# A gated mix of an S4 convolution and a squared-ReLU layer, forward and backward: the whole kernel written anew around a list scheduler

## The chip, the core and the metric

The kernel runs on one core of a Trainium2 chip. The metric is the device time of one execution in microseconds (us). The engines are named as the profile names them: PE is the matrix engine (PEld its weight loads), DVE the vector engine, ACT the scalar engine, POOL the engine that also issues software DMAs, and SP the engine that here only issues DMAs. The core's 16 DMA engines are shared by all queues.

## The reference

One sequence of L = 2048 rows with D = 448 channels, N = 256 states per channel and F = 1792 hidden units. The result is the output and the gradients of all 14 parameters and inputs, 15 tensors in all.

```python
x = A_u;  g = sigmoid((x * gate_w).sum(-1))
# S4: a kernel K(d, l) of exponentials, and a long convolution
dt = exp(log_dt);  logdA = dt * (A_re + 1j A_im);  dB = dt * (B_re + 1j B_im)
l  = arange(L).astype(bfloat16)              # positions are rounded
K  = einsum("dn,dnl,dn->dl", C, exp(logdA[:, :, None] * l), dB).real
a  = irfft(rfft(pad(u)) * rfft(pad(K)))[:L] + u * Dskip
# dense
h  = relu(x @ w1 + b1);  b = (h * h) @ w2 + b2
out = g * a + (1 - g) * b
# returned: out and the vector-Jacobian product with grad_out
```

Because positions are rounded to bfloat16, only some positions above 256 are distinct. Both kernels write a position as an offset plus a step, and get exp(logdA l) as the product of two tables: X over the offsets, Y over the steps. K is then a matmul of X and Y over the states, and the gradients of the S4 parameters come from the gradient of K by the same tables.

## The kernel before

**Convolution.** The transform is two matmul stages forward (`fwd1` L233, `fwd2` L254) and two back (`inv1` L285, `inv2` L303), with the spectra passing through DRAM (`gd`, `sp`, `hd`) between them. A product of two spectra is four multiplies and two adds on DVE (L268, L271 and others). At the start the kernel transforms u and the gradient, which gives the gradient of K in the rounded positions.

**S4 loop.** 13 offsets (`AOFF`) by 64 steps; 14 chunks of 32 channels, in the loop `for c in range(NCH + 1)`. For each chunk DVE builds X (`step_x`: two multiplies L707 and L708, an add L711) and Y (`double`: L718, L719, L721). `kgen` (L772) makes K by matmuls of 64 steps by 16 columns, and `k_out` stores it in `k_d`. For the gradient X is turned by PE (`tables_t` L798, copied by ACT at L799) and Y by PE (`turn_yt` L810, L811) or by a DMA transpose of SP (`load_yt` L818). `back_z` multiplies the turned Y with the gradient of K (L840), ACT copies the result to SBUF (L844), and `back_p` (L860) multiplies it with X on DVE, two products of 2048 elements, and adds up over offsets by matmuls with a selection matrix (L869). The loop interleaves chunk c's tables with the gradient of chunk c - 1:

```python
for c in range(NCH + 1):
    ...
        ax = build_x(c)
        XTs[c] = [tables_t(c, 0)]
    if c > 0:
        ap = back_p(c - 1, XTs[c - 1][0], back_z(c - 1, YTs[c - 1], (0, 1)), (0, 1), ax)
    ...
            ay = build_y(c, half, ap or ax)
```

**Dense branch.** `hidden` (L551, L554) and the gradient of the hidden layer (L1004 to L1015) run over blocks of 512 rows, `project` (L931) over rows of 128; the blocks `rT_d` and `dhT_d` go to DRAM. They are PE's filler while DVE builds tables.

**Order.** Up to about L1030 the tile framework orders the instructions by the pools' buffers and by priorities. The last part is written out by hand: the generator `units()` loads rows of r and dh (`rows_in` L1039), turns them on PE (`turn` L1044, evacuated L1048), multiplies them (`mul_rows` L1057) and turns the results back (`turn_back` L1074), and steps of it are put between those of the transform of K. That part also reloads K (L1125, L1143), loads the spectra of the products (`load_hs` L294) and the dense branch's rows (L1298), stores the outputs (L1412, L1420, L1422, L1435), and has the parameters' gradients on 128 channels at a time (L1155 to L1202).

Of the kernel before, what the change touches and what calls it, by code (L numbers as in the profile page):

```python
# [19 lines left out]
P = 128  # L20
# [3 lines left out]
DT = 4  # L24
DSZ = [128, 128, 128, 64]
DP = 512
CW = 8
NG = 4
CC = NG * CW
NCH = D // CC  # L30
GC = 2
W2 = 2 * CC
NLEV = 11
RS = 1920
NA = 16
AOFF = [0, 1, 2, 3, 256, 258, 512, 768, 1024, 1280, 1536, 1792, 2048]
VA = len(AOFF)
VROW = 2052
# [64 lines left out]
def position_row(v):  # L103

    m, l0 = (v >> 6) & 3, v & 63
    if v < 512:
        return ((v & 3) >> 1, 8 * (l0 >> 2) + 2 * m + (v & 1)) if v < 256 else (2, 8 * (l0 >> 2) + 2 * m + ((v & 3) >> 1))
    if v < 1024:
        return 3, 8 * (l0 >> 2) + 2 * m + ((v - 512) >> 8)
    return (4, 16 * (l0 >> 3) + 4 * m + ((v - 1024) >> 8)) if v < L else (5, 0)  # L110


def sum_consts():

    mats = {}
    k1 = np.arange(32)
    for l, v in enumerate(rounded_positions()):
        l0 = l % 64
        C = (2.0 / 4096) * np.exp(2j * np.pi * (k1 + 0.5) * l / 4096)
        e, row = position_row(int(v))  # L120
        M = mats.setdefault((l0 % 8, l0 // 16, e, row // 32), np.zeros((2, 32, 2, 32)))
        M[l0 // 8 % 2, :, 0, row % 32] += C.real
        M[l0 // 8 % 2, :, 1, row % 32] -= C.imag
    keys = sorted(mats)
    return np.concatenate([mats[k].reshape(128, 32) for k in keys], axis=1), keys


def rev_dim(ap, k):
    dims = [list(x) for x in ap.ap]
    step, cnt = dims[k]  # L130
    off = ap.offset + step * (cnt - 1)
    dims[k] = [-step, cnt]
    return bass.AP(tensor=ap.tensor, offset=off, ap=dims)


def bcast_dims(ap, spec):

    dims = [list(x) for x in ap.ap]
    out = [dims[0]]
    for s in spec:  # L140
        if isinstance(s, tuple):
            out.append([0, s[1]])
        else:
            out.append(dims[1 + s])
    return bass.AP(tensor=ap.tensor, offset=ap.offset, ap=out)


def sel_host_consts():

    sel = np.zeros((128, 4, 48), np.float32)  # L150
    for i in range(8):
        for a in range(VA):
            r = NA * i + a
            sel[r, 0, 16 + 2 * i] = 1.0
            sel[r, 0, 16 + 2 * i + 1] = 1.0 * AOFF[a]
            sel[r, 2, 16 + 2 * i + 1] = 1.0
    sel[:, 1] = -sel[:, 0]
    sel[:, 3] = -sel[:, 2]
    return sel.reshape(128, 192)

class Ker:
    def __init__(self, tc, pool, psum):
        self.tc = tc
        self.nc = tc.nc
        self.pool = pool
        self.psum = psum
        self.evac_i = 0  # L170
        self.st_i = 0
        self.st_more = []
        self.q2 = tc.nc.gpsimd
        self.q3 = tc.nc.scalar
        self.pair_i = 0
        self.pairs = 3
        self.act_only = False
        self.stage_i = 0
        self.dma_i = 0
        self.n = 0  # L180

    def t(self, tag, shape, dt=bf16, bufs=None):
        self.n += 1
        kw = {} if bufs is None else {"bufs": bufs}
        return self.pool.tile(shape, dt, tag=tag, name=f"{tag}_{self.n}", **kw)

    def ps(self, tag, shape, dt=fp32, bufs=1):
        self.n += 1
        return self.psum.tile(shape, dt, tag=tag, name=f"ps{tag}_{self.n}", bufs=bufs)
# [1277 lines left out]
```

## Time and profile before

| what | value |
| --- | --- |
| runs | 960.9, 983.67, 950.6 us; median 960.9 |
| profiled execution, span | 982.7 us |
| PE / DVE / ACT / POOL busy | 717.6 / 689.9 / 563.8 / 222.4 us |
| mean DMA traffic | 185.60 MB, 189 GB/s |
| last store of K (`k_d`) issued by SP | 698.07 us |

The profile is of one execution. Its span is what the instructions and DMAs of the program cover; the time of that same execution is not listed apart, and among the three runs the one of 983.67 us lies nearest to it. In a row of groups the name left of the arrow is what the instruction writes, the shape follows, then the count, the busy time in us, the mean duration in ns, and the idle time of the engine before these instructions with what ended it.

### The profile page before, as it was taken

To read this page: it belongs to the slowest core of one execution; us is meant where nothing else is said; L and a number is where in the kernel's file an instruction comes from. 1 tells how busy PE (TensorE), PEld (TensorE's weight loads), DVE (VectorE), ACT (ScalarE), POOL (GpSimd) and SP (SyncE) were. 2 spreads that over 40 slices of the span, in tenths; PEclk is the share of its full clock that TensorE was granted. 3 is DMA by queue.
4 is the path that set the end of the run, shared out by engine and by line. 5 is a ranking of instruction groups with operands and counts; after the bars stand their busy time and mean duration, and the time that the engine had idled before them with its cause. 6 is when DMAs were issued, how large, how long until landed. Compare 5 with 4: busy or idle time off the path is not lost. (4 is left out here: it accounts for less than half of the span.)

```text
span 982.7 us, 18887 instructions
## 1 busy us (share of the span) xinstructions
PE 717.6 (73%) x7593; PEld 348.2 (35%) x7593; DVE 689.9 (70%) x1184; ACT 563.8 (57%) x873; POOL 222.4 (23%) x364
## 2 busy tenths in 40 slices
PE   3866456786887587887858688399629688787785
PEld 1322111253433244444333344144415344344242
DVE  4797888648889367978958779489319695675362
ACT  0997467548677467766736456255525487344452
POOL 1340001310121012133132433123324221122112
PEclk9967555797988787896979989788958799899798
DMA  9899746961765866767394955954498999898851
GB/s 189 239 280 346 268 184 245 282 194 55 150 146 138 143 126 120 152 171 166 89 147 120 210 128 150 117 121 118 99 292 239 355 293 302 256 281 256 201 151 33
DMA packets 154354, 185.60 MB, mean 189 GB/s; under 512 B 90900, under 2 KB 127050, under 8 KB 153610
## 3 DMA queue, kind: packets, MB, share of 16 engines
q1 hardware_dynamic: 121158, 85.38, 38.5%
q0 software_dynamic: 24880, 76.81, 27.5%
q10 hardware_dynamic: 8228, 22.20, 6.6%
q8 instruction: 59, 0.97, 0.4%
q14 instruction: 29, 0.24, 0.1%
HBM read 95.13 MB, written 68.97 MB: 167 GB/s over the span
## 5 line engine op out<-in xcount | busy, mean ns | idle before, releaser
L931 PE MATMUL psN<-D,S 128*128 128x448 bf16 x448 | 107.7, 384 | 7.3 <-ACT S L1009 4.5
L844 ACT CAST R<-psF 128x1024 bf16<-128x1024 f32 x56 | 57.0, 1018 | 30.6 <-PE psF L840 30.1
L718 DVE TENSOR_TENSOR Y<-Y,F 128x256 bf16<-128x256 bf16 (+2 forms) x84 | 72.7, 866 | 2.3
L721 DVE TENSOR_TENSOR Y<-Y,F 128x256 bf16<-128x256 bf16 (+2 forms) x84 | 72.6, 865 | 2.1
L860 DVE TENSOR_TENSOR P<-R 128x2048 bf16<-128x2048 bf16 x42 | 50.0, 1219 | 34.1 <-ACT R L844 34.1
L719 DVE TENSOR_TENSOR F<-Y,F 128x256 bf16<-128x256 bf16 (+2 forms) x84 | 71.9, 856 | 0.3
L931 PEld LDWEIGHTS <-S 128*128 128x128 bf16 x448 | 42.3, 103 | 56.3 <-issue 24.1
L1057 PEld LDWEIGHTS <-S 128*128 128x128 bf16 x448 | 43.6, 102 | 51.7 <-issue 23.3
L840 PE MATMUL psF<-R,K 64*32 64x256 bf16 (+1 forms) x672 | 27.6, 345 | 43.6 <-DMA R<-Y 23.9
L1057 PE MATMUL psX<-U,S 128*128 128x448 bf16 x224 | 52.5, 382 | 7.4 <-DVE U L1147 6.1
L1004 PE MATMUL psN<-S,U 128*128 128x512 bf16 x168 | 49.0, 414 | 5.4 <-ACT S L1009 5.4
L1057 PE MATMUL psX<-D,S 128*128 128x449 bf16 x224 | 50.2, 370 | 1.6 <-ACT S L1063 1.3
L707 DVE TENSOR_TENSOR X<-X,F 128x512 bf16<-128x512 bf16 (+1 forms) x70 | 37.5, 536 | 18.0 <-ACT F L741 15.8
L799 ACT COPY R<-psX 128x1024 bf16<-128x1024 bf16 x28 | 28.4, 1015 | 35.5 <-PE psX L798 34.0
L1048 ACT ACTIVATE S<-psN 128x1024 bf16<-128x1024 bf16 x28 | 28.8, 1028 | 31.8 <-PE psN L1044 31.8
L811 ACT COPY M<-psX 128x1024 bf16<-128x1024 bf16 x26 | 26.4, 1015 | 33.5 <-PE psX L810 33.5
L933 POOL DMA_DIRECT2D br_d<-D x32 | 17.7, 554 | 117.7 <-ACT D L932 115.9
L772 PE MATMUL psX<-X,Y 128*64 128x16 bf16 x1792 | 38.8, 181 | 7.1 <-issue 6.4
L551 PE MATMUL psN<-S,U 128*128 128x512 bf16 x120 | 37.0, 423 | 7.6 <-ACT S L557 4.6
L772 PEld LDWEIGHTS <-Y 128*64 128x64 bf16 x1792 | 36.3, 119 | 17.6 <-issue 12.5
L840 PE MATMUL psF<-R,S 64*32 64x256 bf16 (+1 forms) x672 | 32.7, 333 | 11.7 <-issue 9.7
L964 ACT ACTIVATE S<-S 128x1024 bf16<-128x1024 bf16 (+1 forms) x24 | 28.2, 1198 | 21.3 <-DMA S<-rT_d 21.3
(336 smaller groups left out, 1795.5 us busy)
## 6 DMA issues: line engine op xcount, KB each, us to landing
sp<-K ACTq DMA_DIRECT2D x8, 896.0 KB, 4.4
S<-rT_d POOLq DMA_DIRECT2D x8, 896.0 KB, 6.8
dhT_d<-S POOLq DMA_DIRECT2D x28, 256.0 KB, 5.3
S<-rT_d POOLq DMA_DIRECT2D x14, 512.0 KB, 6.7
R<-sp SPq DMA_DIRECT2D x8, 896.0 KB, 10.6
S<-dhT_d POOLq DMA_DIRECT2D x14, 512.0 KB, 4.9
R<-hd SPq DMA_DIRECT2D x16, 448.0 KB, 6.5
rec<-rec_d SPq DMA_DIRECT2D x14, 480.0 KB, 4.3
```

The lines of the kernel that those rows point to most:

```text
L551: T_.matmul(ps[:], lhsT=w1w[:, dt, j * P:j * P + P], rhs=UT[:, dt, 512 * lc:512 * lc + 512], start=(dt == 0), stop=False, skip_group_check ...
L707: V.tensor_tensor(out=hi4, in0=lo, in1=bcast_dims(pr, [0, (None, n), 1]), op=ALU.mult)
L718: V.tensor_tensor(out=hi, in0=lo, in1=bcast_dims(pr, [0, (None, n // 2), 1]), op=ALU.mult)
L719: V.tensor_tensor(out=Vv.rearrange("p (x a q) -> p x a q", x=rows, q=2), in0=lo, in1=bcast_dims(pi, [0, (None, n // 2), 1]), op=ALU.mult)
L721: return V.tensor_tensor(out=T4[:, :, :, n:2 * n], in0=T4[:, :, :, n:2 * n], in1=V4, op=ALU.add)
L772: T_.matmul(ps[64 * jt:64 * jt + 64, ch * NA:ch * NA + NA], lhsT=Y[:, w, t, :], rhs=XW[:, 1 - t, w, :, 1], start=(k == 0), stop=(k == 3), ...
L840: T_.matmul(psz[32 * ii:32 * ii + m, t, 256 * s:256 * s + 256], lhsT=(DK[64 * t:64 * t + 64, ro, d] if s == 0 else DKB[64 * t:64 * t + 64, ...
L844: S.copy(zb[:, :, :, gg].rearrange("p s t n -> p t s n"), psz[:].rearrange("p t (s n) -> p t s n", s=2))
L860: lastp = V.tensor_tensor(out=pr.rearrange("p s t g n -> p s t (g n)"), in0=zv, in1=(xb if r == 0 else rev_dim(xb, 2)), op=ALU.mult)
L931: T_.matmul(ps[:, 0:D], lhsT=hblk[j][:, P * tt:P * tt + P], rhs=ws[:, j, :], start=(w == 1 and j == 0), stop=(j == FT - 1))
L1004: T_.matmul(ps[:], lhsT=w2Tw[:, jp, dt, j % 2], rhs=dblk[:, dt], start=(dt == 0), stop=False, skip_group_check=True)
L1057: T_.matmul(ps[:, 0:w], lhsT=hn[i % 2][:, t, :], rhs=(DB2[:, t, :] if i < FT else U[:, t, 0:w]), start=(t == 0), stop=(t == LT - 1))
```

## The change

The whole file is new. All instructions are first recorded as tasks with a duration, a rank and the parts of buffers that they read and write. `schedule()` then goes through time: whenever an engine is free it starts the ready task of the least rank, gives its buffers an address in one SBUF tile (`arena`) or in one of eight PSUM banks (`banks`), and notes the order. Tasks with ranks from 900 on are filler (the dense branch), and DMAs with ranks above 19 wait until the DMA time already given out is within 1 us. The instructions are then written in that order under `manual_schedule`, so that each engine's order is fixed. All of PE's matmuls have one line (L1530), its transposes L1532, DMA transposes L1534, activations L1538, copies and DMAs L1540, other elementwise work L1542.

In the S4 loop 21 offsets by 32 steps take the place of 13 by 64, and 7 chunks of 64 channels the place of 14 of 32. The C·dB factor W goes into X (`XP`), K is 256 matmuls of 32 steps by 42 columns per chunk, all of Y is turned by DMA (four transposes of 128x2048 per chunk) and X is not turned. The gradient works on halves of a chunk: 32 matmuls give Z, six ACT copies bring it to SBUF, two multiplies of 128x5376 on DVE make the products (the first into `XP`, the second in place), and 84 matmuls with the identity or its negative add the 21 offsets in PSUM. Products of spectra are two multiplies of 3584; their adds are done in `inv1` by eight matmuls where there were four.

The dense branch works on blocks of 256 rows. u and the gradient come turned from DRAM by DMA transposes of 128x1024, w1 too; r is squared before its store in `r2_d`. In the last stage rows of `r2_d` and `dh_d` come by 28 DMA transposes of 128x2048 and go straight into the matmuls, so nothing is turned on PE; dW1 is computed with u as the weights and needs no turning back. `U2` and `DB2` are loaded again as rows. The parameters' gradients run over four or three chunks at once.

```diff
-CC = NG * CW
-NCH = D // CC
...
-NA = 16
-AOFF = [0, 1, 2, 3, 256, 258, 512, 768, 1024, 1280, 1536, 1792, 2048]
+NCK, GK = 7, 16
+OFFS = [0, 1, 2, 3, 4, 5, 6, 7, 258, 260, 262, 516, 772, 256, 512, 768, 1024, 1280, 1536, 1792, 2048]
+NA = len(OFFS)
...
+NZ = 1
...
+def schedule(R, total, verbose=0):
...
+                if t.kind == "d" and rk > DMA_RANK and dma_free > now + DMA_LIM + 1e-6:
+                    kept.append((rk, i))
...
+    def product(A, B):
+        T1, T2 = R.buf("T1", 3584), A
+        a = A.v(0, [[896, 4], [D, 2], [1, D]])
+        for T, o in ((T1, 0), (T2, D)):
+            tt(T.v(0, [[896, 4], [D, 2], [1, D]]), a, B.v(o, [[896, 4], [0, 2], [1, D]]), MUL)
+        return T1, T2
...
+    def step(T, st, dst, n, src, ss, rec, lev):
+        lo, hi = T.v(4 * src, [[st, 64], [4 * ss, n], [1, 4]]), T.v(4 * dst, [[st, 64], [4, n], [1, 4]])
+        tt(hi, lo, rec.v(512 * lev, [[4, 64], [0, n], [1, 4]]), MUL)
+        tt(Vt.v(0, [[4 * n, 64], [4, n], [1, 4]]), lo, rec.v(512 * lev + 256, [[4, 64], [0, n], [1, 4]]), MUL)
+        h2 = T.v(4 * dst, [[32 * st, 2], [st, 32], [1, 4 * n]])
+        tt(h2, h2, Vt.v(128 * n, [[-128 * n, 2], [4 * n, 32], [1, 4 * n]]), ADD)
...
+        for (dst, n, src, ss, lev) in ((2, 2, 0, 1, 1), (4, 4, 0, 1, 2), (8, 3, 2, 2, 3), (11, 2, 4, 5, 4), (14, 2, 0, 13, 4), (16, 2, 0, 13, 5), (18, 2, 14, 1, 5), (20, 1, 16, 1, 5)):
+            step(X, 84, dst, n, src, ss, rx, lev)
...
+        for k in range(4):
+            step(Y, 128, 2 << k, 2 << k, 0, 1, ry, k + 1)
+        R.rank = r0 + 26
+        for s in range(2):
+            tt(XP.v(84 * s, [[168, 64], [4, NA], [1, 4]]), X.v(0, [[84, 64], [4, NA], [1, 4]]), W4.v(512 * c + 256 * s, [[4, 64], [0, NA], [1, 4]]), MUL)
...
-        nc.sync.dma_start_transpose(out=YT.rearrange("p h i n -> p (h i) n"), in_=Y[:, 16 * g:16 * g + 16].rearrange("p w t b -> p (w t b)"))
+                R.dma(YTs[h].v(2048 * t, [[128, 16], [1, 128]]), Y.v((2 * t + h) * 2048, [[1, 2048]]), HW, transpose=True)
...
-                lastp = V.tensor_tensor(out=pr.rearrange("p s t g n -> p s t (g n)"), in0=zv, in1=(xb if r == 0 else rev_dim(xb, 2)), op=ALU.mult)
+        tt(P0.v(5376 * h, zv), Z.v(0, zv), X.v(1344 * h, [[0, 2], [2688, 2], [1, 1344]]), MUL)
+        tt(Z.v(0, zv), Z.v(0, zv), X.v(1344 * h + 2688, [[0, 2], [-2688, 2], [1, 1344]]), MUL)
...
+            for t in range(2):
+                for a in range(NA):
+                    mm(ps.f(128 * r, [[1, 128]]), (negI if r == 0 and t == 1 else ident).v(0, [[1, 128]]), T.v(o + 1344 * t + 4 * a, [[2688, 2], [84, 16], [1, 4]]),
+                       t == 0 and a == 0, t == 1 and a == NA - 1)
...
-        for tt in range(8):
-            T_.transpose(ps[:, tt, :], hr[i % 3][:, (8 * th + tt) * P:(8 * th + tt + 1) * P], ident[:])
+        R.dma(T.v(0, [[128, 16], [1, 128]]), d(r2_d, j * P * L, [[L, P], [1, L]], [("r2",)]), HW, transpose=True)
...
+            mm(ps.f(0, [[1, D]]), T.v(128 * t, [[1, 128]]), DB2.v(D * t, [[1, D]]), t == 0, t == LT - 1)
...
+            R.dma(T.v(2048 * i, [[128, 16], [1, 128]]), d(dh_d, j * P * L, [[L, P], [1, L]], [("dh",)]), HW, transpose=True)
...
+    with tc.manual_schedule():
+        for i in order:
+            e, calls = R.tasks[i].used
```

What the change makes of the order is shown at two places. The first is DVE's list in the S4 loop. Before, a piece of one chunk: the last steps of Y (L718, L719, L721 on the Y table with F as scratch), two of the gradient's multiplies (L860, from the ACT copy R into P and M), and the start of the next chunk's X.

```order
L718 TENSOR_TENSOR Y_205_1605<-Y_205_1605,F_207_1608 128x64x32
L719 TENSOR_TENSOR F_207_1608<-Y_205_1605,F_207_1608 128x2048
L721 TENSOR_TENSOR Y_205_1605<-Y_205_1605,F_207_1608 128x64x32
L860 TENSOR_TENSOR P_209_1611<-R_208_1610 128x2048
L860 TENSOR_TENSOR M_210_1612<-R_208_1610 128x2048
L728 COPY X_206_1606<-rec_3473 128x128x4
L707 TENSOR_TENSOR X_206_1606<-X_206_1606,F_207_1608 128x128x4
```

After, DVE's list at the end of a chunk's tables (all SBUF is `arena`, all PSUM `banks`): the last step of Y, XP (128x64x84), the sum of K's two halves (8x21), the two products of the gradient's first half (5376 x2), pieces of the dense branch (1024) and of the next chunk's gradient of K (672), and the two products of the second half.

```order
L1542 TENSOR_TENSOR arena<-arena 128x64x64
L1542 TENSOR_TENSOR arena<-arena 128x64x84 x2
L1542 TENSOR_TENSOR arena<-banks,arena 128x8x21
L1542 TENSOR_TENSOR arena<-arena 128x5376 x2
L1542 TENSOR_TENSOR arena<-banks,arena 128x8x21
L1542 TENSOR_TENSOR arena<-arena 128x1024
L1542 TENSOR_SCALAR arena<-arena 128x672 x4
L1542 TENSOR_TENSOR arena<-arena 128x5376
L1542 TENSOR_TENSOR arena<-arena 128x1024 x2
L1542 TENSOR_TENSOR arena<-arena 128x5376
```

The tables of a chunk of 64 channels and its gradient now stand as one block each; the gradient's products are 5376 long, and its second half comes after a gap that holds only short pieces.

The second place is SP's list in the last stage. Before, it held plain loads of the spectra (`hd`) and rows (`br_d`) and the stores of the output.

```order
L294 DMA R32_540_8789<-hd2 64x4x896 x4
L1298 DMA R32_540_8789<-br_d 128x2x448 x2
L1412 DMA out_1_dram<-F17_538_8752 32x2x896 x4
L294 DMA R32_540_8789<-hd2 64x4x896 x2
L1412 DMA out_1_dram<-F17_538_8752 32x2x896 x4
L294 DMA R32_540_8789<-hd2 64x4x896 x2
```

After, in the middle of that stage, where the transform of K is stored (`gd2`) and the first products go back (`hd1`):

```order
L1540 DMA gd2<-arena_61 64x4x448
L1540 DMA arena_61<-gd2 128x3584 x3
L1540 DMA arena_61<-st_d 128x2048
L1534 DMA_TRANSPOSE arena_61<-r2_d 128x16x128 x5
L1540 DMA arena_61<-gd2 128x3584
L1540 DMA hd1<-arena_61 64x4x448
L1534 DMA_TRANSPOSE arena_61<-r2_d 128x16x128
L1540 DMA hd1<-arena_61 64x4x448
```

DMA transposes of r² now stand in SP's queue ahead of the fourth load of `gd2` and of stores of `hd1`.

More of the change, by code (lines that the diff above doesn't have):

```diff
@@ L1 @@
+import heapq
 import math
-from contextlib import ExitStack, nullcontext
 import ml_dtypes
@@ L288, in inv1 @@
[L288 to L305 removed]
+                ps = R.ps("i1", 2)
@@ new lines, in build @@
+    b1f = R.buf("b1f", 32, top=True)
+    ps = R.ps("b1")
+    R.rank = 25.0
+    R.group("PE")
+    R.op("PE", "transpose", out=ps.v(0, [[1, FT]]), in_=prow.v(0, [[1, P]], 0, FT), ident=ident.v(0, [[1, FT]], 0, FT))
+    R.end()
+    V("tensor_copy", out=b1f.f(0, [[1, FT]]), in_=ps.v(0, [[1, FT]]))
+    DB = R.buf("DB", 8192)
+    R.rank = 31.0
+    for t in range(LT):
+        scaled(DB.v(512 * t, [[1, D]]), G.v(D * t, [[1, D]]), omg32.f(t, [[1, 1]]))
+    V("tensor_copy", out=DB.v(448, [[512, 16], [1, 64]]), in_=DB.v(384, [[512, 16], [1, 64]]))
```

2418 lines of the change are left out of this document (1242 added, 1176 removed).

## The prediction

> **What bounds the kernel now.** I read the page from the top (busy shares, then the 40 slices), then cut the span into its three stages with the windows view.
>
> ```profile
> PE 717.6 (73%) x7593; PEld 348.2 (35%) x7593; DVE 689.9 (70%) x1184; ACT 563.8 (57%) x873; POOL 222.4 (23%) x364
> ...
> PE   3866456786887587887858688399629688787785
> ...
> DVE  4797888648889367978958779489319695675362
> ...
> DMA  9899746961765866767394955954498999898851
> ```
> No engine is busy over 73% of the span, so the limits must change from stage to stage. The DMA row shows it: nines at both ends, fives to sevens between.
>
> ```profile
> 0.00:188.00 188.00, 112.40 (x479) 39.95 (x479) 142.44 (x315) 124.53 (x215) 35.33 (x52) 0.68 0.80 252
> 188.00:698.00 510.00, 398.07 (x5579) 203.06 (x5578) 387.07 (x560) 304.23 (x423) 118.27 (x190) 0.85 0.66 138
> 698.00:982.70 284.70, 207.10 (x1538) 105.16 (x1537) 160.35 (x310) 135.07 (x236) 68.82 (x123) 0.87 0.81 237
> ```
> The columns are the window, its length, busy time of PE, PEld, DVE, ACT and POOL, the granted clock, the DMA share and GB/s. Stage A (0 to 188) is the forward transforms and the seeds; stage B (188 to 698) the S4 loop with the dense work as filler; stage C (698 to the end) the transform of K, the outputs and the dense weight gradients. The cut at 698 is the last store of K (an issue of SP, 698.07). In A and C the DMA engines are busy 0.80 and 0.81. In B PE has 398 of 510 us and DVE 387, which hand one chunk to and fro:
>
> ```profile
> 213.57 0.29 DVE L728 COPY X<-rec 128x512 bf16<-128x512 bf16 x1
> 224.93 0.43 DVE L707 TENSOR_TENSOR X<-X,F 128x512 bf16<-128x512 bf16 x1 [11.06 <-ACT F L741]
> ...
> 254.64 0.29 DVE L728 COPY X<-rec 128x512 bf16<-128x512 bf16 x1 [2.09 <-PE psX L772]
> ```
> Line 728 opens a chunk of 32 channels. This one took 41 us with its wait for ACT; the mean is 510/14 = 36.4 us, so 72.9 us for 64 channels.
>
> **The change part by part. Stage B, DVE.** The price list of an elementwise multiply:
>
> ```profile
> L718 DVE TENSOR_TENSOR Y<-Y,F 128x2048 bf16<-128x2048 bf16 x42 | 51.4, 1223 | 0.9
> ...
> L860 DVE TENSOR_TENSOR P<-R 128x2048 bf16<-128x2048 bf16 x42 | 50.0, 1219 | 34.1 <-ACT R L844 34.1
> ...
> L707 DVE TENSOR_TENSOR X<-X,F 128x512 bf16<-128x512 bf16 x56 | 28.7, 512 | 17.5 <-ACT F L741 15.8
> ...
> L711 DVE TENSOR_TENSOR X<-X,F 128x512 bf16<-128x512 bf16 x56 | 23.8, 424 | 1.4
> ...
> L718 DVE TENSOR_TENSOR Y<-Y,F 128x1024 bf16<-128x1024 bf16 x14 | 9.7, 693 | 0.5
> ```
> From 693 to 1223 ns for 1024 more elements: 0.52 ns each and 0.16 us for the instruction. L707 reads runs of two elements, L711 longer ones; the difference is 88 ns. L718 (also runs of two) and L860 (long runs) cost the same. So per chunk of 64 channels afterwards: X, eight steps, 3 x 4096 elements in 24 instructions: 6.4 + 3.9, with L707's 88 ns on 16 of them 11.7, say 12 us. Y, 3 x 7680 in 12: 13.9. XP, 2 x 5376: 2 x 2.95 = 5.9. The gradient's two products for each of two halves: 4 x 2.95 = 11.8. Sum 43.6 us. Before, DVE spent 387/7 = 55.3 us per 64 channels in this stage, all work counted.
>
> DVE cannot run these without a pause. XP is overwritten by the gradient's first products, so it waits for the K matmuls that read XP; and the second half's products wait for sums and new Z in PSUM.
>
> ```profile
> L772 PE MATMUL psX<-X,Y 128*64 128x16 bf16 x1792 | 38.8, 181 | 7.1 <-issue 6.4 <-DVE Y L721 0.4 <-ACT R L811 0.3
> ...
> L1044 PE MATMUL psN<-ident,S 128*128 128x128 bf16 x224 | 18.7, 230 | 0.0
> ...
> L931 PE MATMUL psN<-D,S 128*128 128x448 bf16 x448 | 107.7, 384 | 7.3 <-ACT S L1009 4.5 <-ACT S L964 2.7
> ...
> L844 ACT CAST R<-psF 128x1024 bf16<-128x1024 f32 x56 | 57.0, 1018 | 30.6 <-PE psF L840 30.1
> ```
> Busy time over count is what PE pays: 22 ns for a K matmul of 16 columns, 83 ns for one of 128, 240 ns for one of 448. K: 256 matmuls, now of 42 columns, 22 to 28 ns: about 6.5 us of wait. Between the halves stand 84 sum matmuls (7 us), and Z, whose six casts of some 900 to 1000 elements take about 1 us each by L844, 6.5 us: if these run one after the other 14 us, if beside each other 7; I take 10. Period 43.6 + 6.5 + 10 = 60 us.
>
> PE has its own sum: K 6, sums 168 x 83 ns = 14, Z 32 x 168 columns about 3, and the dense filler. A block of 256 rows is 56 matmuls of 256 columns (137 ns, scaled from L931) and 28 of 448: 7.7 + 6.7 = 14.4 us; 16 blocks over 7 chunks make 33. Sum 56 us per 60. So PE is nearly as long as DVE, and 56 us (both perfect) to 66 us (PE at 0.85 use) are the bounds of the period. The first tables take 12 + 14 + 6 + 6 = 38 us before K(0). **Stage B: 38 + 6 x 60 = 398 us** against 510 (374 to 434).
>
> What is removed besides: the PE turns of X and of part of Y (lines 798 and 810) with their copies on ACT, and half of ACT's casts. ACT falls from 564 to about 436 us (its instructions at the durations of before); it holds no long wait then, and I cost this at nothing beyond the period.
>
> **The transposes.** This is the part that costs. Added up from the programs' instructions, there are 42 DMA transposes before and 80 after (28 of Y, 16 blocks for the dense part, 28 of rows of r² and dh, 8 of weights and inputs); 20 MB become 36 MB. Plain traffic falls from 164 to 150 MB.
>
> ```profile
> q1 hardware_dynamic: 6240, 1.57, 67.9%
> q0 software_dynamic: 371, 1.19, 23.8%
> ...
> R<-Y SPq DMA_TRANSPOSE x3, 7.2
> ```
> This is the DMA view of 246 to 262 us. All of queue q1's 1.57 MB are three transposes of Y: 0.679 x 16 us = 10.9 us of all engines, 3.6 us each, 144 GB/s. Plain traffic shares the same engines: 67.9% and 23.8% add up.
>
> ```profile
> q1 hardware_dynamic: 79174, 28.52, 34.8%
> q0 software_dynamic: 13408, 40.68, 30.0%
> ```
> Over 188 to 698 queue q1 takes 0.348 x 510 = 177 us for 28.5 MB. 36 transposes are 18.9 MB of it; the other 9.6 MB at q0's rate (40.68 MB in 153 us, 266 GB/s) are 36 us, which leaves 141/36 = 3.9 us each.
>
> The Trainium skill, "DMA: Bandwidth & Descriptors", section "Latency and other measured facts", gives a DMA transpose 261 GB/s effective. The trace does not agree: 144 GB/s. By the page the 28 transposes of stage C would take an estimated 56 us and not 101 to 109, and the kernel some 50 us less than I forecast.
>
> In stage B the new kernel moves about 52 MB plain and the equal of 39 transposes: 52/0.266 + 39 x 3.9 = 348 us of 398. Hidden, but with little to spare.
>
> **Stage A.** DMA share 0.80 at 252 GB/s, 47 MB. The new program moves about 45 MB up to the S4 loop: 143 us at full share (315 GB/s), 179 at 0.80. DVE has some 100 us in place of 142 (its instructions at the prices above), since adds of spectra went into PSUM. I take **165 us**, 23 less.
>
> **Stage C.** Turning r and dh on PE (L1044) goes, and their plain loads; instead SP issues 28 transposes.
>
> ```profile
> 800.00:850.00 50.00, 41.24 (x292) 20.72 (x292) 33.83 (x41) 29.98 (x45) 7.00 (x13) 0.93 0.98 314
> ...
> 950.00:982.70 32.70, 21.91 (x150) 11.56 (x147) 13.66 (x37) 10.17 (x25) 6.85 (x12) 0.90 0.14 40
> ```
> At 0.98 the engines moved 314 GB/s, and the last 33 us are nearly free of DMA. Before that, (0.81 x 284.7 - 0.14 x 32.7)/252 = 0.90 of the time. Afterwards 50.4 MB plain remain behind the last store of K: 50.4/0.314 = 160 us. 28 transposes at 3.6 to 3.9 us: 101 to 109. Sum 265 us, at 0.90 use 295, and the tail: the last group of 64 matmuls (256 columns, 9 us) and a store, 12 us. **Stage C: 306 us**, 22 longer than before. The added waits stand on SP, which holds its queue while it issues:
>
> ```profile
> L818 SPq DMA_TRANSPOSE R<-Y x36: 1582/3636/12004, 247.8 to 658.5; - x36
> ...
>   PE psF L840: 23.9, 7
> ...
> 925.81 18.13 DMA R<-hd x2
> ```
> The first row gives least, median and greatest time of one such instruction on SP's queue: 3.6 us, up to 12. Behind a run of five of them the order has a load of gd2 and the stores of hd1, on which the conv waits; and with two buffers each of the five also waits for the dW2 matmuls of the one but last. Already before, a load of hd took 18 us on the chain that ended last. PE's work there is not the bound: 207 us less 37 for the turns, plus some 15 for doubled inverse matmuls, about 185 of 306.
>
> **Sum.** 165 + 398 + 306 = 869 us of span against 982.7. That execution lies by the slowest of the three runs (983.67); the median 960.9 is 0.978 of it: 869 x 0.978 = **850 us**, 11% faster. The runs spread over 3.4%; about 2% is what a measurement here can tell from no change.
>
> **Rivals.** 1. Transposes from DRAM are cheaper than those from SBUF that the trace shows; its least instruction was 1.58 us. 28 x 1.6 = 44 us, DMA 204/0.90 + 12 = 239, and with PE at its best use in a stage (0.78) 185/0.78 = 237. The whole: 165 + 398 + 238 = 801, or 165 + 374 + 238 = 777 with the shorter period; 760 to 783 in the median's frame, say **772**. The three transposes of 246 to 262 us speak against it, that r² and dh come in whole rows of 4096 bytes for it. The 261 GB/s of the Trainium skill, "DMA: Bandwidth & Descriptors", would bear it out.
> 2. The slower side: the order is fixed, each engine obeys it, and the dense blocks stand on PE ahead of K or Z. Each waits for a transpose that SP issues in a queue with four of Y: 12 us at the worst of L818. With 2.3 blocks a chunk that is 28 us a chunk, 6 x 28 = 168: 1037 us, 1014 in the median's frame; half of it gives 930. It decides from 19 us a chunk ((982.7 - 869)/6). For it: SP has 4 x 3.6 + 2.3 x 1.8 = 18.5 us of transposes in each period. Against: before, PE lost only 23.9 us in 7 waits to such transposes. Its time: **1000**.
> 3. DVE loses its rate on runs of four elements, of which the new tables have 34,300 per chunk: 240,000 x 0.52 ns = 125 us more, 994 x 0.978 = **972**, within 2%. L718 with runs of two at full rate speaks against it.
> That the work is not removed is excluded: the order lists 635 instructions on DVE where 1148 stood, and 6517 matmuls for 7593.
>
> **How the numbers follow.** Forecast 0.48 (own range 800 to 905: stage B's bounds, A 143 to 179, C by 3.6 to 3.9 us and use 0.85 to 0.95), rival 1 0.27, rival 2 0.16, rival 3 0.05, still faster than 735 by both stages at their best 0.04. Faster by over 2%: 0.48 + 0.27 + 0.04 and a hundredth of rival 2, 0.80; within 2%: rival 3 and 0.06 of rival 2, 0.11; slower: the rest of rival 2, 0.09. From 735 to 955 all but about 2 in 10 lies.
>
> **What would show it.** Right: seven pairs of 5376-element products on DVE per half with a period near 60 us; the last store of K near 563; DMA nines from there on, transposes of r² and dh at 3.6 us and over 280 us to the end. Rival 1: such transposes near 1.6 to 2 us, PE and not DMA filling the last stage. Rival 2: periods over 80 us, with PE idle behind a DMA at a dense block. Rival 3: 2048-element work of the tables over 2 us. I am wrong also if stage A does not shrink, since its seeds and stores stand in a new order.

## The result, and the profile after

The changed kernel takes 1025.87 us (median of four runs, 1023.0 to 1029.28). The kernel before took 970.82 us in the same comparison (median of four). Two of its four runs (980.73 and 983.67 us) were slow executions, and the ratios, here and in all that follows, are formed without such runs. The ratio is 1.0731, with a 95% interval of 1.0669 to 1.0793: the changed kernel is slower by 7%, where I had forecast 850 us.

The page's first part of the changed kernel, and its DMA row over 40 slices:

```profile
PE 754.6 (74%) x6519; PEld 400.4 (39%) x6519; DVE 527.3 (52%) x667; ACT 426.2 (42%) x597; POOL 184.8 (18%) x305
...
DMA  9799899846681472577446437337797599999971
```
The work on DVE and ACT fell (690 to 527 us, 564 to 426; for ACT I had reckoned with 436). PE did not get shorter but longer, 718 to 755 us, with 1074 matmuls fewer. That is the first thing to ask about.

The windows of the changed kernel, with the columns as before. K(0) is the first K of the S4 loop, at 260 us. The windows are the first 200 us, then from K(0) to the last store of K (715), then from there to the end:

```profile
0.00:200.00 200.00, 80.46 (x574) 35.61 (x575) 97.08 (x149) 107.29 (x118) 44.06 (x75) 0.77 0.90 276
260.00:715.00 455.00, 398.52 (x4061) 227.48 (x4062) 274.59 (x316) 182.44 (x277) 47.56 (x72) 0.81 0.52 127
715.00:1021.00 306.00, 236.71 (x1475) 116.77 (x1473) 125.95 (x163) 105.71 (x147) 82.68 (x141) 0.83 0.81 215
```
| stretch | forecast, us | measured, us |
| --- | --- | --- |
| start to K(0) | 165 + 38 = 203 | 260 |
| K(0) to the last store of K | 360 | 455 |
| last store of K to the end | 306 | 306 |

So 152 us were missed in the first two stretches. In the second, PE is busy 399 of 455 us. Groups of the changed kernel, by shape:

```profile
L1530 PE MATMUL banks<-arena 128*128 128x168 bf16 x448 | 142.8, 493 | 1.0 <-ACT arena L1540 1.0
...
L1542 DVE TENSOR_TENSOR arena<-arena 128x5376 bf16<-128x5376 bf16 x42 | 123.7, 2954 | 51.3 <-ACT arena L1540 28.6 <-PE banks L1530 22.2
...
L1530 PE MATMUL banks<-arena 128*128 128x128 bf16 x1176 | 79.5, 231 | 10.9 <-DVE arena L1542 10.9
...
L1542 DVE TENSOR_TENSOR arena<-arena 128x4096 bf16<-128x4096 bf16 x21 | 47.6, 2288 | 4.0 <-DMA arena<-dk_d 3.7
...
L1530 PE MATMUL banks<-arena 128*32 128x42 bf16 x1792 | 23.1, 222 | 44.5 <-issue 24.8 <-DVE arena L1542 19.6
...
L1542 DVE TENSOR_SCALAR arena<-arena 128x672 bf16<-128x672 bf16 x24 | 7.9, 391 | 86.6 <-PE banks L1530 86.6
```
Busy time over count is again what one matmul costs PE. The first row is Z: 142.8/448 = 319 ns for 168 columns, 1.9 ns a column. The 128-column sums take 68 ns and the 42-column K matmuls 13. The last row is the scaled copies that write the next chunk's gradient of K over the one that Z reads. One chunk on PE's timeline, on DVE's, and as a window:

```profile
540.33 2.44 PE L1530 MATMUL banks<-arena 128*32 128x42 bf16 x198 [3.39 <-DVE arena L1542]
545.20 73.61 PE L1530 MATMUL banks<-arena 128*32 128x42 bf16 x542 [2.42 <-issue]
622.21 2.71 PE L1530 MATMUL banks<-arena 128*32 128x42 bf16 x225 [3.40 <-DVE arena L1542]
```
```profile
542.38 0.92 DVE L1542 TENSOR_TENSOR arena<-banks,arena 128x168 bf16<-128x168 f32 x1 [1.15 <-ACT arena L1540]
...
567.90 1.31 DVE L1542 TENSOR_SCALAR arena<-arena 128x672 bf16<-128x672 bf16 x4 [15.02 <-PE banks L1530]
...
624.22 0.95 DVE L1542 TENSOR_TENSOR arena<-banks,arena 128x168 bf16<-128x168 f32 x1 [1.12 <-ACT arena L1540]
```
```profile
542.38:624.22 81.84, 75.74 (x760) 43.65 (x749) 50.52 (x61) 29.90 (x41) 9.28 (x14) 0.85 0.48 124
```
The 168-element add of K marks the chunk: 81.8 us from one to the next, against 60 in the forecast. PE is busy 75.7 us of them, 73.6 without a pause, and between the two halves DVE waits 15 us for Z before it may write the scaled copies.

The stretch before K(0), on DVE:

```profile
195.72 0.36 DVE L1540 COPY arena<-arena 128x768 bf16<-128x768 bf16 x1 [24.32 <-DMA arena<-rec_d]
...
213.69 0.23 DVE L1540 COPY arena<-arena 128x256 bf16<-128x256 bf16 x1 [6.28 <-DMA arena<-dk_d]
...
220.75 4.13 DVE L1542 TENSOR_TENSOR arena<-arena 128x512 bf16<-128x512 bf16 x9 [3.77 <-DMA arena<-dk_d]
...
233.33 8.15 DVE L1542 TENSOR_TENSOR arena<-arena 128x2048 bf16<-128x2048 bf16 x5 [8.45 <-DMA arena<-dk_d]
...
245.13 8.03 DVE L1542 TENSOR_TENSOR arena<-arena 128x4096 bf16<-128x4096 bf16 x3 [3.65 <-DMA arena<-dk_d]
...
260.39 0.91 DVE L1542 TENSOR_TENSOR arena<-banks,arena 128x168 bf16<-128x168 f32 x1 [3.83 <-ACT arena L1540]
```
The row at 260.39 is K(0). The four ahead of it are the first copy into Y and its steps, which read no byte of `dk_d` (the gradient of K), and yet they wait 22 us in all for its loads. Other work that shares no data with these loads is held too. The first row below is one of the loads on POOL, which waits for PE; the second, on ACT, squares r for the dense branch and waits 10 us for a load:

```profile
209.18 0.90 POOL L1540 DMA_DIRECT2D arena<-dk_d  x1 [5.88 <-PE banks L1530]
...
220.76 1.70 ACT L1538 ACTIVATE arena<-arena 128x1792 bf16<-128x1792 bf16 x1 [9.96 <-DMA arena<-dk_d]
```
There are four such loads, and each writes every fourth partition of `arena`. My suspicion was that a write of this form counts as a write to far more than it touches.

### The profile page after: what moved, and what is told of

Its sections match the earlier page's. It is cut to its first block, busy times and chain, and to the rows that moved or that the text cites. A ratio compares the mean times of both kernels' runs of the same rounds, so it can differ in the third digit from the quotient of the medians.

```text
span 1021.2 us, 15733 instructions
## 1 busy us (share of the span) xinstructions
PE 754.6 (74%) x6519; PEld 400.4 (39%) x6519; DVE 527.3 (52%) x667; ACT 426.2 (42%) x597; POOL 184.8 (18%) x305
## 5 line engine op out<-in xcount | busy, mean ns | idle before, releaser
L1530 PE MATMUL banks<-arena 128*32 128x42 bf16 (+11 forms) x6400 | 741.7, 312 | 246.1 <-DVE arena L1542 71.2
L1530 PEld LDWEIGHTS <-arena 128*128 128x128 bf16 (+5 forms) x6396 | 390.7, 109 | 592.7 <-issue 414.7
L1542 DVE TENSOR_TENSOR arena<-arena 128x512 bf16<-128x512 bf16 (+15 forms) x439 | 420.7, 999 | 170.8 <-ACT arena L1538 45.7
L1540 ACT CAST arena<-banks 128x896 bf16<-128x896 f32 (+6 forms) x303 | 237.0, 835 | 332.7 <-PE banks L1530 306.7
L1538 ACT ACTIVATE arena<-arena 128x1792 bf16<-128x1792 bf16 (+8 forms) x60 | 65.5, 1105 | 38.9 <-DMA arena<-dk_d 13.7
L1542 DVE TENSOR_SCALAR arena<-arena 128x448 bf16<-128x448 bf16 (+6 forms) x69 | 23.0, 393 | 102.5 <-PE banks L1530 102.5
L1540 ACT COPY arena<-banks 128x168 f32<-128x168 f32 (+4 forms) x43 | 22.3, 533 | 115.6 <-PE banks L1530 99.4
L1540 POOL DMA_DIRECT2D out_dram<-arena x66 | 36.0, 548 | 139.9 <-ACT arena L1540 130.9
L1538 ACT ACTIVATE arena<-banks,arena 128x256 bf16<-128x256 f32 (+1 forms) x117 | 46.5, 488 | 20.0 <-PE banks L1530 12.8
L1540 POOL DMA_DIRECT2D br_d<-arena x30 | 16.5, 550 | 168.3 <-ACT arena L1540 168.1
L1538 ACT ACTIVATE arena<-banks 128x1024 bf16<-128x1024 f32 (+1 forms) x32 | 29.1, 915 | 42.0 <-PE banks L1530 40.6
L1540 DVE COPY arena<-arena 128x256 bf16<-128x256 bf16 (+5 forms) x18 | 8.3, 464 | 65.4 <-DMA arena<-rec_d 34.2
L1542 DVE SCALAR_TENSOR_TENSOR arena<-arena 128x448 bf16<-128x448 bf16 (+3 forms) x38 | 33.9, 953 | 13.8 <-PE banks L1530 12.8
L1542 DVE TENSOR_TENSOR arena<-banks,arena 128x168 bf16<-128x168 f32 x14 | 12.9, 921 | 40.3 <-ACT arena L1540 40.3
L1540 POOL DMA_DIRECT2D hd<-arena x34 | 21.4, 633 | 52.4 <-ACT arena L1540 50.3
L1540 POOL DMA_DIRECT2D gd<-arena x30 | 18.8, 628 | 59.4 <-ACT arena L1540 57.4
L1540 POOL DMA_DIRECT2D r_d<-arena x16 | 13.2, 823 | 90.4 <-ACT arena L1538 64.7
L1540 ACT COPY arena<-arena 128x256 bf16<-128x256 bf16 (+3 forms) x34 | 22.2, 680 | 7.7 <-DMA arena<-rec_d 5.9
L1540 POOL DMA_DIRECT2D dh_d<-arena x8 | 8.9, 1106 | 90.6 <-DVE arena L1542 90.6
L1542 DVE SCALAR_TENSOR_TENSOR arena<-banks,arena 128x448 bf16<-128x448 f32 x32 | 18.6, 648 | 11.5 <-PE banks L1530 9.7
L1532 PE MATMUL banks<-arena 128*128 128x128 bf16 (+2 forms) x119 | 13.4, 262 | 11.5 <-ACT arena L1540 6.3
L1540 POOL DMA_DIRECT2D rec_d<-arena x10 | 9.5, 953 | 52.1 <-DVE arena L1540 39.1
```

The lines of the kernel that those rows point to most:

```text
L1530: fn(out, **kw)
L1532: fn(out, kw["in_"], kw["ident"], **({"tile_position": kw["tile_position"]} if "tile_position" in kw else {}))
L1538: fn(out, kw.pop("in_"), kw.pop("func"), **kw)
L1540: fn(out, kw["in_"])
L1542: fn(out=out, **kw)
```

## The experiments

Each kernel is the changed one with the edit shown, unless another base is named. Medians are of four runs (ten for e2); ratios are to the kernel before on the same chip, whose median lay between 953.9 and 957.3 us.

**Z: how its columns are read.** Theory Z holds that the reading of the gradient of K makes Z slow; its rival, that PE's fixed order and clock set the period anyway.

```diff
-mm(ps.f(512 * k + 84 * gi, [[84 * ng, 2], [4, NA], [1, 4]]), ..., B.v(g, [[336, 2], [16, NA], [672, 4]]), True, True)
+mm(ps.f(512 * k + 84 * gi, [[84 * ng, 2], [1, 4], [4, NA]]), ..., B.v(g, [[336, 2], [672, 4], [16, NA]]), True, True)
```
Expected of e1:

> Edit: the Z matmuls take their 168 columns in another order (channel of the group outermost, offset innermost), so that consecutive columns are 32 bytes apart in DKB and not 1344; the results land at the same places of PSUM. Order, bytes and counts as in the changed kernel. Theory Z (Z is slow by how it reads its moving operand, 319 ns for 168 columns where the rows of before make 90): if the long distance is the cause, 90 to 110 ns each, 448 x 0.22 = 95 us less on PE, the period from 81 to about 65 us, 925 to 945 us in all. If any read of single elements is the cause, 319 ns stays and 1026 us. Rival (PE's fixed order and its clock set the period, Z only fills it): Z gets shorter, PE waits instead, 1005 to 1026 us.

998.65 us, ratio 1.0432 (1.039 to 1.0473). Z hardly moved:

```profile
L1530 PE MATMUL banks<-arena 128*128 128x168 bf16 x448 | 137.8, 482 | 1.0 <-ACT arena L1540 1.0
```
That is 308 ns with 32 bytes between columns, against 319 with 1344, so of my two cases for Z it is the one in which any read of single elements is dear. I had put that case at 1026 us; the 27 us below it came from elsewhere, as the last section tells.

Then the 168 columns of a Z matmul were laid out in one run:

```diff
-scaled(DKB.v(672 * c4, [[16, 42], [1, 16]]), dKc...
+scaled(DKB.v(c4, [[4, 42], [168, 16]]), dKc...
...
-B.v(g, [[336, 2], [16, NA], [672, 4]])
+B.v(168 * g, [[84, 2], [4, NA], [1, 4]])
```
Expected of e2:

> Edit: DKB is laid out so that the 168 columns of a Z matmul lie in one run; the four scaled copies that fill DKB write single elements 8 bytes apart instead of a run. Theory Z: 90 ns per Z matmul, 95 to 100 us less on PE; the copies grow from 0.39 to up to 0.9 us on DVE, 2 us per chunk; 930 to 950 us. Rival (fixed order and clock): 1005 to 1030 us.

953.72 us, ratio 0.9955 (0.9911 to 0.9998): level with the kernel before, 72 us less than the changed one. Its groups:

```profile
L1530 PE MATMUL banks<-arena 128*128 128x168 bf16 x448 | 41.3, 243 | 10.1 <-ACT arena L1540 6.4 <-DVE arena L1542 3.6
...
L1542 DVE TENSOR_SCALAR arena<-arena 128x672 bf16<-128x672 bf16 x24 | 37.5, 1876 | 40.5 <-PE banks L1530 40.5
```
Z takes 41.3/448 = 92 ns: the distance of the columns was its price. But the copies now write single elements 336 bytes apart (16 in a row; the 8 bytes that I had expected are the step of their outer loop), and rose on DVE from 391 to 1876 ns.

**The loads of dk_d.**

```diff
-    for c4 in range(4):
-        R.dma(dKc.v(0, [[112, 42], [1, 112]], c4, 32, ps=4), d(dk_d, 112 * c4, [[D, 32], [32 * D, 42], [1, 112]], ...
+    for i, (a0, na) in enumerate(((0, 11), (11, 11), (22, 10), (32, 10))):
+        R.dma(dKc.v(112 * a0, [[112, na], [1, 112]]), d(dk_d, 32 * D * a0, [[112, 128], [32 * D, na], [1, 112]], ...
```
Expected of e3:

> Edit: the gradient of K is loaded by four DMAs that each write all 128 partitions and a quarter of the offsets, in place of four that each write every fourth partition; same bytes, same packets. Theory D (between 206 and 246 us the tables of chunk 0 wait for these loads, which themselves wait for everything before them, only because a store to every fourth partition counts as a store to all of them): the waits of 6.3, 3.8, 8.5 and 3.7 us on DVE go, K(0) stands 20 to 26 us earlier, 1000 to 1006 us. Rival (the DMA engines are busy 0.9 there and the seeds come late anyway): within 8 us of 1026.

1007.95 us, ratio 1.0542 (1.0482 to 1.0602), 18 us less. DVE's timeline:

```profile
205.45 23.42 DVE L1542 TENSOR_TENSOR arena<-arena 128x512 bf16<-128x512 bf16 x25
230.42 4.34 DVE L1542 TENSOR_TENSOR arena<-arena 128x512 bf16<-128x512 bf16 x8 [1.55 <-issue]
240.66 0.99 DVE L1542 TENSOR_TENSOR arena<-banks,arena 128x168 bf16<-128x168 f32 x1 [5.91 <-ACT arena L1540]
```
Y runs through and K(0) stands at 240.7 instead of 260.4, and the time is 2 us above the range that I gave. Theory D holds: those waits had no cause in the data.

The first and this edit together:

Expected of e4:

> Edit: the first and the third together. Both theories: the sum of both gains, 900 to 925 us. Rivals: 990 to 1026 us.

979.17 us, ratio 1.0233 (1.0181 to 1.0285): 47 us less, about the sum of 27 and 18, but far from the 900 to 925 expected, as Z was still 308 ns.

**A layout that serves both sides.** The rows of e3, and:

```diff
+scaled(DKB.v(c4, [[64, 42], [4, 16]]), dKc...
...
+B.v(4 * g, [[64 * NA, 2], [64, NA], [1, 4]])
```
Expected of e5:

> Edit: the rows of e3, and DKB laid out by offset, group, channel, so that a Z matmul reads runs of four columns, 128 bytes from run to run; the scaled copies write single elements 8 bytes apart, with 16 of them to a run of 128 bytes (in e2 they jumped 336 bytes and took 1.88 us on DVE and 3.39 on ACT instead of 0.39 and 0.85). Theory Z with the price on every column that isn't next to the last one: 42 of 168 columns pay, 92 + 42 x 1.35 ns = 150 ns; with the price on the length of the run alone (runs of four as in the sums and in K, which pay nothing): 92 to 100 ns. Copies by theory W (their price in e2 is the jump of 336 bytes): 0.4 to 0.9 us. Time: e2's 954 less 20 for the rows and 20 to 35 for the copies: 900 to 915 us. Rival (the period hangs on PE's dense filler, the copies were hidden): 930 to 940.

929.18 us, ratio 0.9738 (0.9661 to 0.9815): some 2 to 3% faster than the kernel before, but 14 us above the range that I gave and next to the rival's 930. Its groups of Z and of the copies, a window of one chunk, and two rows of the timelines of DVE and SP:

```profile
L1530 PE MATMUL banks<-arena 128*128 128x168 bf16 x448 | 40.6, 237 | 7.2 <-ACT arena L1540 6.7 <-DVE arena L1542 0.5
...
L1542 DVE TENSOR_SCALAR arena<-arena 128x672 bf16<-128x672 bf16 x24 | 19.3, 964 | 42.6 <-PE banks L1530 42.6
```
```profile
480.31:548.56 68.25, 57.94 (x758) 39.73 (x750) 52.34 (x61) 29.73 (x41) 8.83 (x14) 0.95 0.60 149
```
```profile
246.73 0.98 DVE L1542 TENSOR_TENSOR arena<-banks,arena 128x168 bf16<-128x168 f32 x1 [8.55 <-ACT arena L1540]
```
```profile
627.41 0.88 SPq L1540 DMA_DIRECT2D k_d<-arena  x2
```
Runs of four columns cost as little as one long run, 91 ns. The window is one chunk: 68 us, DVE busy 52.3 and PE 57.9. The last two rows are K(0) and the last store of K: the second stretch is now 381 us, and with a span of 925.6 us the third 298.

**Columns 16 bytes apart.** With the rows of e3, and scaled copies that write runs of eight; first in e1's column order, then in the changed kernel's own:

```diff
+B.v(g // 8 * 336 + g % 8, [[8 * NA, 2], [672, 4], [8, NA]])     # channel outermost
+B.v(g // 8 * 32 + g % 8, [[64 * NA, 2], [64, NA], [8, 4]])      # offset outermost
```
Expected of e12:

> Edit: e4 (rows; Z's columns with the channel outermost), with DKB laid out so that consecutive columns of a Z matmul are 16 bytes apart and not 32; the scaled copies write runs of eight. Theory Z as the runs stand so far (single elements 1344 or 32 bytes apart cost 308 to 319 ns per 168 columns, single elements 8 bytes apart nothing, as in K): the limit lies between 8 and 32 bytes. If 16 bytes pay as 32 do: 308 ns and e4's 979 us. If the price grows with the distance: 150 to 200 ns and 940 to 955. If 16 bytes are free: 90 ns and 915 to 930.

980.95 us, ratio 1.025 (1.0187 to 1.0314); Z 136.8/448 = 305 ns. Here as in e1 PSUM was also written with a step, so one more run was needed:

Expected of e13:

> Edit: the rows of e3, and DKB laid out so that the columns of Z are read in their first order (offset outermost, channel innermost), the four channels 16 bytes apart and the offsets 128; the results go to PSUM one behind the other as in e5. In e1, e4 and e12 the results were also written to PSUM 16 bytes apart, so those runs don't tell a slow read from a slow write. Theory R (the read of single elements is what costs, from some step between 8 and 16 bytes on): 300 to 310 ns per Z matmul and 975 to 1010 us. Theory S (there the step in PSUM cost, and reads cost only at 1344 bytes): 90 to 95 ns, and, with copies of 0.39 us, 915 to 930 us.

1005.11 us, ratio 1.0575 (1.0514 to 1.0636).

```profile
L1530 PE MATMUL banks<-arena 128*128 128x168 bf16 x448 | 141.8, 491 | 0.7 <-ACT arena L1540 0.7
```
317 ns with PSUM written in one run: it is the read. Single elements 16, 32 or 1344 bytes apart cost 305 to 319 ns.

The expectation of e12 takes it that single elements 8 bytes apart cost nothing, since K reads its columns so at 13 ns for 42. That row doesn't show it. K's matmuls are 32 weight columns wide and the kernel puts them side by side at four places of the array; 13 ns for 42 columns are 0.31 ns a column, less than the 0.54 that Z pays in one run, so they must overlap. Four of them take 4 x 13 = 52 ns, which allows up to 1.2 ns a column for each. A step of 8 bytes costs less than the 1.9 ns of 16 bytes; whether it is free, no run tells.

**What sets the period now.** On e5, eight matmuls of each row block of the dense branch's projection (`pj`) are left out, so that its results are partial sums:

```diff
+            if R.tasks[i].name == "pj":
+                calls = calls[:6] + calls[-1:]
```
Expected of e8:

> Edit: e5, with 8 of the 14 or 15 matmuls of each row block of the projections left out (the first six and the last stay; their results are then partial sums). 32 x 8 x 0.23 = 59 us less on PE, nearly all in the S4 stage; nothing else moves. Theory P (PE's sum is the period: 56 us or more of work per chunk in the fixed order): the period falls by 7 to 8 us, 45 to 55 us in all. Rival V (DVE's chain with its two waits is the period, the filler stands in PE's pauses): 0 to 15 us.

910.49 us, ratio 0.9537 (0.9458 to 0.9617), 19 us less than e5 with its full filler: between both theories. One chunk:

```profile
471.13:536.62 65.49, 50.36 (x705) 35.44 (x693) 52.21 (x61) 29.66 (x41) 8.85 (x14) 0.92 0.65 154
```
PE gave up 7.6 us of this chunk, and the chunk became 2.8 us shorter. So PE's filler holds a part of the period. I take it that DVE's chain, 52 us of work and its waits, holds the rest.

**The first stretch.** The seeds' load of chunk 0 was moved from SP's queue to ACT's, on e5:

```diff
+    order.remove(R.rx0.i)
+    order.insert(1 + max(order.index(x) for x in R.rx0.deps), R.rx0.i)
+    R.rx0.used = ("ACT", R.rx0.used[1])
```
Expected of e7:

> Edit: e5, with the first load of X's seeds (rec_d to rx for chunk 0) issued by ACT right behind the last store of its seeds, and not by SP, where it stands behind the loads of hd0 and a store of dk_d. Nothing else moves. Theory Q (the S4 loop starts late because that load waits in SP's queue: DVE idles 24.3 us for it): X of chunk 0 starts 15 to 22 us earlier and the kernel ends 12 to 22 us earlier. Rival (PE needs its time in the S4 stage anyway, with all the dense work in it, so an earlier start is lost in later waits): 0 to 5 us.

923.73 us, ratio 0.9672 (0.9593 to 0.9751); K(0) at 246.5 against 246.7. Theory Q falls. Lines of POOL, ACT's queue and DVE:

```profile
168.30 1.00 POOL L1545 DMA_DIRECT2D rec_d<-arena  x1
...
181.20 0.41 ACTq L1545 DMA_DIRECT2D arena<-rec_d  x1
...
195.49 0.36 DVE L1545 COPY arena<-arena 128x768 bf16<-128x768 bf16 x1 [21.88 <-DMA arena<-rec_d]
```
The load went out 13 us after the seeds' last store and came in 14 us later. It is not the place in SP's queue; the way through DRAM takes 27 us, in which (168 to 195.5 us) the DMA engines are busy 0.97.

Then, on e5, three stores of 2.1 MB into scratch tensors (`extra`) were added to the stretch, ahead of the store of `db_d`:

```diff
+                    for x in extra:
+                        eng[e].dma_start(bass.AP(tensor=x, offset=0, ap=[[8192, P], [1, 8192]]), real(kw["in_"]))
```
Expected of e9:

> Edit: e5, with three more stores of 2.1 MB each into scratch tensors that nobody reads, issued by POOL right ahead of the store of db_d (about 100 us from the start). Theory B (the first stage is as long as its bytes: 55 MB in the first 200 us at 0.9 of the DMA engines' time, where I had reckoned with 45): 6.3 MB more take 6.3/0.305 = 21 us, K(0) comes at 263 to 270 instead of 247, and the end 16 to 22 us later. Rival (a chain of waits between the engines sets the first stage, DMA has gaps to spare): K(0) within 6 us of 247.

937.6 us, ratio 0.9848 (0.9762 to 0.9935). K(0), on DVE:

```profile
255.90 0.91 DVE L1547 TENSOR_TENSOR arena<-banks,arena 128x168 bf16<-128x168 f32 x1 [4.48 <-ACT arena L1545]
```
6.3 MB more put it off by 9 us, not 21. The first stretch is bound by its bytes in part only.

**The last stretch.** On e5, the 28 transposes of r² and dh are made plain loads of the same bytes, which leaves out the turning, so that the weight gradients are formed of wrong data:

```diff
+                elif name == "dma_start_transpose" and kw["in_"].tensor.name in ("r2_d", "dh_d"):
+                    nc.sync.dma_start(out, kw["in_"].rearrange("p (a b) -> p a b", b=128))
```
Expected of e6:

> Edit: e5, with the 28 DMA transposes of r2_d and dh_d in the last stage made plain loads of the same bytes at the same places of the order (the rows are then not transposed, so dW1 and dW2 are of wrong data; all else is the same). Theory T (the last stage is as long as its DMA time, and a transpose takes 3.7 us where a plain load of 0.52 MB takes 1.7): 28 x 2.0 = 56 us less DMA and 28 x 3 us less of SP's queue: the last stage falls by 45 to 60 us. Rival (the chain of the transform of K, the parameters' gradients and the weight gradients on PE sets it): 0 to 15 us.

921.74 us, ratio 0.9637 (0.9566 to 0.9707): 7 us less, where theory T gave 45 to 60. The windows near the end with transposes, then without:

```profile
820.00:860.00 40.00, 33.31 (x195) 13.31 (x196) 5.83 (x18) 11.28 (x21) 10.45 (x19) 0.86 0.92 217
860.00:900.00 40.00, 35.25 (x164) 15.62 (x165) 0.00 (x0) 6.60 (x11) 7.59 (x14) 0.96 0.87 180
```
```profile
820.00:860.00 40.00, 35.42 (x212) 13.82 (x213) 8.13 (x27) 13.09 (x23) 11.29 (x20) 0.91 0.73 244
860.00:900.00 40.00, 39.28 (x182) 18.30 (x183) 0.00 (x0) 6.43 (x11) 8.13 (x16) 1.00 0.48 173
```
The DMA share falls from 0.87 to 0.48 and the time hardly changes: PE works through what is left of the weight gradients, nearly alone. Over the whole last stretch the DMA share is 0.82 of 298 us in e5 and 0.70 of 289 here: some 42 us of DMA time less, of which the stretch gained 9. So I moved the weight gradients ahead in the list. This kernel is e5 with e7's edit and:

```diff
-        R.rank = FR + 81 + j
+        R.rank = 412.5 + 0.01 * j
...
-            R.rank = FR + 97 + j
+            R.rank = 415.5 + 0.01 * j
```
Expected of e10:

> Edit: e5 with the seeds' load by ACT as in e7, and the ranks of the two weight gradients put between the parameters' gradients and the outputs (412.5 and 415.5 instead of 981 to 1014), so that the list scheduler starts them ahead of most of the last transforms; its order is made anew from the last chunk on. Theory S (in the last stage the weight gradients come too late: SP issues their transposes behind stores that wait for the parameters' gradients, and PE ends with some 85 us of them with nothing beside): the last stage falls from 291 to 298 us to 260 to 280, 895 to 910 us in all. Rival T2 (the DMA engines are full there at 0.9, whatever the order): within 8 us of e7's 924; and if the outputs now come too late in their turn, slower, up to 940.

905.97 us (893.93 to 922.66), ratio 0.941 (0.9306 to 0.9514), the fastest kernel here: 6% under the kernel before. The last stretch fell from 298 to 275 us. SP's queue in the changed kernel (start, length, instructions), and in this one:

```profile
715.04 0.88 SPq L1540 DMA_DIRECT2D k_d<-arena  x2
...
938.52 3.89 SPq L1534 DMA_TRANSPOSE arena<-dh_d  x1
...
958.95 37.18 SPq L1534 DMA_TRANSPOSE arena<-dh_d  x10
```
```profile
627.80 0.87 SPq L1545 DMA_DIRECT2D k_d<-arena  x2
...
796.01 31.22 SPq L1539 DMA_TRANSPOSE arena<-dh_d  x8
```
Counted from the last store of K, the transposes of dh now begin after 168 us; in the changed kernel they began after 223, in e5 after 217. Theory S holds. In the windows from 680 to 780 us the DMA engines are now busy 0.97: with the order mended, the DMA times begin to count.

## Why the prediction was wrong, point by point

**Z's term was mis-sized; it is the step that failed.** The prediction gave "Z 32 x 168 columns about 3" us of PE per chunk. A chunk has 64 such matmuls, 32 for each half, and each took 319 ns: 20.4 us. Of the 17 us missed, 3 are the half that I had not counted, and 14 to 15 are the price of one. With 20.4 in place of 3, PE's sum of 56 us a chunk becomes 73; the window shows 75.7, and PE, not DVE, sets the 81.8 us. Half of Z stands in DVE's gap between the halves, for which I had taken 10 us. I had scaled a price per column from rows whose columns lie side by side, without reading where the columns of this operand lie. With the rows and the layout of e5 the second stretch fell from 455 to 381 us, against 360 forecast, and the total by 97. These 74 us are not all Z's own time. In e12 Z still takes 305 ns, but the granted clock of the stretch is 0.93 where the changed kernel and e13 have 0.81 and 0.80, and the stretch takes 420 us (241.9 to 662.2) where e13 takes 453 (242.6 to 696.0). So some 33 us went with the clock, which the last section takes up, and some 40 (420 to 381, e5 at 0.90) with the price of Z, although the scaled copies became dearer.

The Trainium skill, "SBUF — State Buffer", section "SBUF: two separate sides", states a mechanism: SBUF answers in lines of 16 bytes, full rate needs at least two hits per line, and each crossing to a new line is penalised. The runs agree where they can tell: Z is cheap with four hits per line, in runs of four (91 ns), and dear with one, at 16 bytes and beyond (305 to 319 ns). Two hits, as K has them, are left open. The same section of the Trainium skill also says that a step of 8 bf16 is free; at that step, 16 bytes, the runs show the full price (305 and 317 ns). The rule of the lines spoke against this change, and I had not weighed it.

**The period.** My 43.6 us of DVE per chunk left out the copies of the gradient of K, the adds of K and the dense branch's products; a chunk has 52.3 us of DVE. The later periods of e5 are some 68 us against 60. From K(0) (246.7) to K(6) (616.6) its six periods take 370 us, 62 on the mean, since the first is only 33: with Z's price right, the forecast of the stretch is nearly met. The prices themselves were right: 5376 elements 2954 ns for 2.95 us forecast, 4096 elements 2288 for 2.29. Rival 3 (runs of four elements lose DVE's rate) is refuted by that.

**The first stretch.** 45 MB were forecast and 0.276 x 200 = 55 MB moved. By e9's 9 us for 6.3 MB, ten more are some 15 us (an estimate from that run). The false waits were 14 to 20 us (K(0) at 246.7 in e5 and at 240.7 in e3, against 260.4). The remaining 22 to 28 of 57 us I put to the seeds' way through DRAM, for which the forecast had nothing; that is argued from one trace and not shown by a run.

**The last stretch: right number, wrong reason.** 306 us came out as 306. But the sum of DMA times behind it was not the bound: 28 plain loads in place of the transposes took 7 us off the kernel. What set it is the order: weight gradients left for the end, on PE nearly alone.

The price of a transpose from DRAM was wrong as well. The row at 958.95, ten of them in 37.18 us, holds pauses between them. SP's instructions themselves, with least, median and greatest time in ns (buffer numbers are left out, so `r_d` stands for `r2_d`):

```profile
L1534 SPq DMA_TRANSPOSE arena<-r_d x14: 1949/2712/9380, 431.5 to 942.5; - x14
L1534 SPq DMA_TRANSPOSE arena<-dh_d x14: 1995/2689/4557, 938.5 to 993.5; - x14
```
That is 2.7 us. In the window from 959 to 996 us queue q1 moved the 5.13 MB of these ten in 0.71 x 37 = 26.3 us of all engines, 195 GB/s, and not 144. So the truth lies between rival 1's 1.6 us and my 3.6 to 3.9. At 2.7 us the forecast's own sum would give (160 + 76)/0.90 + 12 = 274 us (an estimate). That 306 came out is luck: prices too high by 32 us in this sum stood in for an order that cost about as much (306 to 275 us in e10).

**Rival 2** forecast a slower kernel with periods over 80 us, and both came. Its mechanism was not at work in the chunk shown: PE did not stand idle behind DMA transposes, it was busy 75.7 of 81.8 us.

## What to carry to other kernels

Before a matmul gets a price, read the steps of its moving operand in bytes: a layout that is handy for the engine that writes it can cost PE three and a half times the work. Where the order is fixed by a list made from a cost table, a wrong price shows in every period, though not in full: from e12 to e5 Z fell by 13.7 us per chunk (64 x 305 less 64 x 91 ns), 96 us over seven chunks, and the stretch by 40, with dearer copies and a clock of 0.90 in place of 0.93. Whether a list made with the true price would have hidden more of it, no run tells. And a write to every n-th partition of a shared tile can bind engines that share no data; look at what waits for such an instruction before trusting the order around it.

## What the runs showed of the hardware that I had not expected

The granted clock went with the order of Z's columns, with nearly the same time per Z matmul. Windows over the middle chunks of the changed kernel, of e1 and of e13:

```profile
391.00:704.00 313.00, 277.17 (x2791) 159.07 (x2780) 193.90 (x226) 111.93 (x154) 33.85 (x52) 0.82 0.52 129
```
```profile
385.00:680.00 295.00, 253.59 (x2872) 152.44 (x2863) 193.88 (x226) 112.98 (x156) 33.86 (x52) 0.94 0.54 138
```
```profile
380.00:690.00 310.00, 273.70 (x2768) 157.77 (x2766) 191.11 (x226) 112.36 (x153) 33.91 (x52) 0.81 0.53 132
```
0.82 and 0.81 with the channel innermost, 0.94 with the offset innermost (308 to 319 ns for Z in all three). At 0.94 the other matmuls are faster. Those of 448 columns, first of e1, then of the changed kernel:

```profile
L1530 PE MATMUL banks<-arena 128*128 128x448 bf16 x816 | 183.3, 372 | 52.3 <-DMA arena<-in_A_u_dram 20.8 <-ACT arena L1540 14.6 <-DMA arena<-r_d 10.2
```
```profile
L1530 PE MATMUL banks<-arena 128*128 128x448 bf16 x816 | 206.3, 407 | 54.4 <-DMA arena<-in_A_u_dram 20.9 <-ACT arena L1540 12.3 <-DMA arena<-r_d 10.7
```
225 ns against 253. Three pairs of kernels that differ in this order (e1 and the changed one, e4 and e3, e12 and e13) are 24 to 29 us apart; the first two pairs differ in nothing else, the third in the layout too. Whether it is the read or the step of 16 bytes in PSUM that goes with it, no run tells, and why the clock answers to either stays open.

Single-element writes are dear too: a scaled copy of 672 elements took 391 ns in runs on DVE (the changed kernel), 964 at 8 bytes apart (e5), 1876 at 336 bytes (e2).
